# An adaLN, H3 and SwiGLU kernel: another written order, other buffer homes, and additions exchanged between VectorE and GpSimd in the front

## The chip, the cores and the metric

The kernel runs on one core of a Trainium2 chip. The time is the device time of one execution in microseconds (us); three timed executions and one profiled execution are shown for the kernel before. A core has TensorE (matmuls, PE in the profile), VectorE (DVE), ScalarE (ACT), GpSimd (POOL) and SyncE (SP). Here SP's queue issues every DMA.

## The reference

The sequence has S = 2048 steps, the model D = 512 channels, the feed-forward net F = 1792. All of it is float32.

```python
mod = silu(c) @ w_mod                       # six vectors of 512: sa, ca, ga, sb, cb, gb
h = layernorm(q) * (1 + ca) + sa
k4 = sum over t of 4 of shift_k[:, t] * k delayed by t        # per channel
kv = k4 * v
y = (causal convolution of kv with ssm_k, 2048 long, by FFT) + kv * ssm_D
x = q + ga * (h * y)
h = layernorm(x) * (1 + cb) + sb
out = x + gb * ((silu(h @ w_gate) * (h @ w_up)) @ w_down)
```

## The kernel before, in words

The kernel has two parts. The main part (lines 1755 to 1806) is a loop over weight tiles of the feed-forward net: matmuls in fp32r with operands split into a high and a low part, and sums of blocks that save one product in eight. The change doesn't touch it. The front, everything before it, is straight code: a list of 513 calls, written out by hand in `adaln_h3_swiglu`, that begins after the definitions, at line 1169.

The channels are worked on in 4 chunks of 128. In chunk 1 the four taps on k are matmuls with small diagonal matrices on TensorE (`conv`); in chunks 0, 2 and 3 they are scaled copies and additions (`tap0`, `tap`, `tap2`), and `times_v` multiplies by v. Then:

- The long convolution is a transform in two steps, of 64 points by matmuls with the table e_fwd (`er` in the profile). `kx_first` and `k_first` do the first step for the kernel ssm_k, `x_first` and `xk_first` for kv. `k_turn` and `xk_turn` turn the result on TensorE. `swap_x` and `swap_k` transpose blocks of 32x32 in place on VectorE, and `put`, `get`, `put_k`, `get_k` transpose by writing to DRAM and reading back. `skip` adds ssm_D to the first value of ssm_k.
- The second step, the product of the spectra and the step back are done in 8 half-chunks n: `x2` makes two forms of x, `x_sum` adds them, `prod` multiplies each with k's form as it leaves PSUM, `inv` goes back. Then swaps again, and `y_pe` does the last step with e_inv (`ei`).
- Beside it run the loads and small matmuls for `mod` (`mod_load`, `mod_rows`, `mod_out`, `mod_in`, `mod_part`, `mod_T`, `mod_mix`), the first layernorm (`do_stats`, `do_aggr`), and `gate_n`, `gate_m`, `gate_a`, which make h from q in half tiles (the normalised rows, times 1 + ca, plus sa, with ga worked in).
- `y_gate` multiplies h by y as it leaves PSUM, `add_y` adds that to x. `stat`, `do_norm2a`, `norm2b`, `norm_t` and `norm_s` are the second layernorm, its transposes on TensorE, and its scaling. `op_hi` and `op_lo` split the result in two parts, `w8_hi` and `w8_lo` split the weights of the first two F blocks; `wd_mul`, `wd_hi` and `wd_lo` do so for the down weights, and `split_w` for the next blocks. `gu_pe`, `gu_act` and `gu_end` are the gate and up products of these two blocks, `diff` and `downs` follow, and then the main loop begins.

What sets the order: every engine runs its instructions in the order of the program (`InOrder`, lines 56 to 64), and the framework inserts the waits between engines. A function marked `@parts` (lines 67 to 76) is a generator: each time its call stands in the list the next part of it is issued, so that `prod(4, 2)` written twice issues its matmuls at the first place and its product from PSUM at the second. So the list of calls is the schedule. SP's queue too is in that order: a load whose buffer isn't free holds up those behind it. SP's first eight loads each have a semaphore of their own, and from the ninth on they are used again.

What sets the buffers: each tile is taken from a pool under a tag with a home, a digit from the strings in `HOMES` (lines 33 to 53), read one by one as the tiles are made:

```python
    def home_of(tag, home=None):
        return f"{tag}_{next(homes[tag]) if home is None else home}"
```

`b16`, `e8`, `r4`, `k2` and `xs` are homes in SBUF, `ps` is one of four pairs of PSUM banks. A tile waits for the last use of the one before it in its home. Just ahead of the main loop another PSUM pool is opened (`next_psum`), after which `downs` writes into its banks.

An addition or product is put on VectorE or GpSimd by an argument of its call:

```python
    def gate_a(t, half, engine=pool):
        s = S1[t][:, 2 * half : 2 * half + 2]
        engine.tensor_tensor(s, s, bcs[:, None, 0, :].to_broadcast([P, 2, D]), op=ALU.add)
```

Of the kernel before, what the change touches and what calls it, by code (L numbers as in the profile page):

```python
# [34 lines left out]
        "2503145354221253044"  # L35
    ),
    "e8": (
        "61037245103724153204326432634623634642623634"
    ),
    "r4": (  # L40
        "10420123403120210433041230421140322041104230143201423104213402143021340213140204020402"
    ),
    "k2": (
        "0210210201020102010201020102010201201201201201201200112"
    ),
    "xs": (
        "10100101"
    ),
    "ps": (
        "2023102121031201321023103203102103120312310213012012012301301302310230120312032103213213210321032102"  # L50
        "31023102310231021031232123032031312"
# [28 lines left out]
def adaln_h3_swiglu(ctx, tc, q, kT, vT, kP, vP, shk, wt, ssm, dskip, wgu, wdn, c, wmod, e_fwd, e_inv, w_c, out, out_t):  # L80
# [1025 lines left out]
    def load_c():  # L1106
        sp.dma_start(csil, c)
# [74 lines left out]
    load_ssm(2)  # L1182
    kx_first(2, 1)
    k_first(0, 3)
    load_k(0, 0)
    load_ssm(0, 0)
    kx_first(2, 2)
    tap0(0, dve, 0)
    load_c()
    skip(2, pool)  # L1190
    load_e(0)
    load_k(0, 1)
    kx_first(2, 3)
    k_first(0, 2)
    kx_first(2, 2)
    skip(0)
    load_kp(1)
    load_v(0, 0)
    load_v(0, 1)
    load_v(0, 3)  # L1200
    tap(0, 1, 0)
    load_v(0, 2)
    tap(0, 2, 0)
    k_first(0, 0)
    tap0(0, dve, 1)
    load_vp(1)
    tap(0, 3, 0)
    k_first(0, 0)
    tap(0, 1, 1)
    tap(0, 2, 1)  # L1210
    kx_first(2, 0)
    tap(0, 3, 1)
    times_v(0, 0)
    times_v(0, 3)
    k_turn(0, 2)
    kx_first(2, 0)
    times_v(0, 2)
    times_v(0, 1)
    kx_first(2, 3)
    kx_first(2, 1)  # L1220
    load_k(2)
    k_turn(0, 3)
    conv(1)
    conv(1)
    conv(1)
    k_turn(0, 3)
    load_v(2)
    load_ssm(1)
    skip(1, pool)
# [12 lines left out]
    x_first(0, 1)
    x_first(0, 2)
    tap0(2, dve)
    tap(2, 1)
    tap(2, 2)
    tap2(2, 3, 1)
    x_first(0, 0)
    x_first(0, 3)
    k_turn(0, 0)  # L1250
    x_first(0, 2)
    x_first(0, 1)
    x_first(0, 3)
# [36 lines left out]
    silu_c()  # L1290
    times_v(2, 3)
    x2(1, 1)
    k_first(1, 3)
    x2(1, 1)
    x_sum(0, dve)
    load_x(1)
    prod(0, 1)
    x2(1, 2)
    x2(1, 2)
    prod(0, 0)  # L1300
    prod(0, 0)
# [72 lines left out]
    do_stats(2, 3)
    do_aggr(0)
    mod_out()
    x2(2, 2)
    x_sum(2)
    skip(3, pool)
    x2(3, 2)  # L1380
    get_k(2, 0, 1)
    x2(3, 1)
    x2(3, 1)
    xk_turn(2, 2)
    xk_turn(2, 2)
    mod_in()
    xk_turn(2, 0)
    x_sum(3)
    get_k(2, 2, 3)
    times_v(3, 2)  # L1390
    times_v(3, 0)
    do_stats(1, 3)
    xk_turn(2, 0)
    xk_turn(2, 3)
    times_v(3, 3)
    do_aggr(1)
    do_aggr(1)
# [12 lines left out]
    do_aggr(0)  # L1410
    do_aggr(0)
    do_stats(2, 2)
    times_v(3, 1, pool)
    prod(3, 2)
    prod(3, 0)
    gate_n(0, 3)
    do_stats(3, 1)
    x_first(3, 2)
    x_first(3, 2)
    gate_n(0, 2)  # L1420
    x_first(3, 3)
    x_first(3, 3)
    xk_turn(2, 1)
    xk_turn(2, 1)
    do_aggr(3)
    do_stats(2, 0)
    do_aggr(1)
    do_aggr(3)
    inv(3)
    put(0)  # L1430
    gate_n(0, 0)
    gate_n(0, 1)
    inv(3)
    inv(3)
    mod_mix()
    inv(2)
    gate_m(0, 0)
    inv(2)
    inv(2)
    x_turn(3, 0)  # L1440
    put(1)
    gate_m(0, 1, dve)
    x2(5, 2)
    do_aggr(2)
    do_aggr(2)
    x_turn(3, 0)
    x2(5, 2)
    x2(5, 1)
    get(0)
    do_aggr(2)  # L1450
    x2(5, 1)
    x_sum(5, dve)
    get(1)
# [24 lines left out]
    k_first(3, 0)
    x_first(3, 1)
    x_sum(4)  # L1480
    prod(4, 1)
    gate_m(3, 0, dve)
    k_first(3, 0)
    swap_x(12)
    k_first(3, 2)
    gate_n(2, 2)
    k_first(3, 2)
    load_einv()
    prod(4, 2)
    prod(4, 0)  # L1490
    prod(4, 2)
    gate_n(2, 0)
    prod(4, 0)
    swap_x(14)
    gate_n(1, 2)
    inv(5)
    swap_x(15)
    swap_x(13)
    gate_m(2, 1)
    gate_n(2, 1)  # L1500
    gate_n(1, 3)
    inv(5)
    gate_n(1, 0)
    inv(5)
    inv(4)
    k_turn(3, 1)
    inv(4)
    gate_m(1, 1, dve)
    gate_a(1, 1, dve)
    k_turn(3, 3)  # L1510
    inv(4)
    k_turn(3, 3)
    put(2)
    gate_a(3, 0, dve)
    gate_a(2, 1)
    gate_a(0, 0)
    gate_m(1, 0, dve)
    gate_a(1, 0, dve)
    k_turn(3, 1)
    k_turn(3, 2)  # L1520
    k_turn(3, 2)
    k_turn(3, 0)
    k_turn(3, 0)
    x2(6, 1)
    load_w(1)
    x2(6, 1)
    x2(7, 2)
    x2(7, 2)
    x2(6, 2)
    x2(7, 1)  # L1530
    prod(6, 0)
    x2(6, 2)
    x2(7, 1)
    get(2)
    gate_n(3, 3)
    gate_a(0, 1)
    x_sum(6, dve)
    prod(6, 0)
    y_pe(0, 0, 1)
    y_gate(0, 0, 1)  # L1540
    prod(7, 0)
    x_sum(7)
    prod(7, 0)
    prod(7, 1)
    prod(7, 1)
    prod(6, 2)
    prod(6, 2)
    prod(7, 2)
    add_y(0, 0, 4, (0, 1), pool)
    prod(7, 2)  # L1550
    prod(6, 1)
    gate_m(2, 0)
    prod(6, 1)
    inv(7)
    inv(7)
    w8_hi(1)
    inv(7)
    gate_a(2, 0)
    inv(6)
    stat(0, 0)  # L1560
    gate_m(3, 1)
    swap_x(14)
    mod_load(3, 4)
    w8_lo(1, pool)
    load_einv2()
    y_pe(0, 2)
# [12 lines left out]
    mod_part(4)
    mod_T(3)  # L1580
    y_gate(1, 0, 1)
    swap_x(12)
    y_pe(0, 3)
    add_y(0, 0, 4, (2,), pool)
    add_y(1, 0, 4, (0, 1), pool)
    stat(0, 1)
    y_gate(0, 3)
    mod_T(3)
    add_y(0, 0, 4, (3,), dve)
    load_w(0)  # L1590
# [299 lines left out]
```

## Time and profile before

| What | us |
|---|---|
| timed runs | 585.79, 586.29, 587.15 |
| their median | 586.29 |
| profiled execution | 587.44 |
| its span in the profile | 585.7 |
| its mean granted TensorE clock | 0.997 of full speed |

In the profile's rows `PE`, `PEld` (weight loads of TensorE), `DVE`, `ACT`, `POOL` and `SPq` name the engines or queues. All instructions recorded by `InOrder` carry line 64, so a group of instructions is told by its tiles: `out<-in` gives the names of the tile that is written and of those read. `kt` is k or its transform, `u` the sum of taps, `vt` v, `s` the half tiles of h, `bcs` the rows from `mod`, `xs` the forms of x, `X`, `T`, `K` the transformed chunks, `y` the last step of the convolution, `n` the normalised rows, `nt` their transposes, `hraw` the scaled rows, `op` the split operands, `g` the gate and up products, `dn` the down products, `a` the first products of the main part. In timeline rows the first number is the start in us from the start of the span, the second the time up to the end of the last instruction of the group, and in brackets stands the idle time before it and what ended it. In grouped rows stand the count, the busy time in us and the mean of one in ns, and then the idle time before.

### The profile page before, as it was taken

What the parts mean: (1) busy time and instruction counts of PE and PEld (TensorE: products, weight loads), DVE (VectorE), ACT (ScalarE), POOL (GpSimd) and SP (SyncE); (2) the same over time, 40 slices, a digit from 0 to 9 for tenths busy, and PEclk for the clock granted to TensorE, in tenths of its full rate; (3) what the DMA queues carried; (4) which work ended last, traced back from release to release, by engine and by line L of the source; (5) the groups of instructions that cost most, each with busy time, mean ns of one, the idle gap of its engine ahead of it and who ended that gap; (6) DMA issues with size and microseconds to landing.
All of it is one profiled execution on the core that took longest, in us unless ns stands there. A gap on an engine that the chain in (4) does not pass through costs nothing.

```text
span 585.7 us, 10169 instructions
## 1 busy us (share of the span) xinstructions
PE 568.5 (97%) x4074; PEld 447.4 (76%) x4074; DVE 447.5 (76%) x599; ACT 293.7 (50%) x440; POOL 341.1 (58%) x256
## 2 busy tenths in 40 slices
PE   3999999999999999999999999999999999999997
PEld 3994554746887888888888888888888888888885
DVE  0999975899796977877778868865577777777775
ACT  2697979954583454337354435435433333333320
POOL 0042565559364596674948794376283837474991
PEclk9999999999899999999999999999999999999999
DMA  8998999999101397191836480075343434343403
GB/s 275 413 404 304 321 177 280 379 300 350 37 37 26 149 367 284 58 355 55 290 138 205 186 304 28 5 267 196 126 162 126 161 127 161 126 161 126 162 2 143
DMA packets 41914, 113.87 MB, mean 194 GB/s; under 512 B 3189, under 2 KB 19973, under 8 KB 36362
## 3 DMA queue, kind: packets, MB, share of 16 engines
q1 hardware_dynamic: 41866, 113.22, 54.2%
q8 instruction: 32, 0.52, 0.4%
q14 instruction: 16, 0.13, 0.1%
HBM read 74.92 MB, written 38.29 MB: 193 GB/s over the span
## 4 chain that ended last, share of the span: by engine, by line
PE 87%; DVE 5%; ACT 4%; DMA 1%; issue 1%; POOL 1%; SPq 1%; ACTq 0%; DVEq 0%
PE dn L64 14%; PE b L64 12%; PE a L64 12%; PE c L64 11%; PE dq L64 10%; PE d L64 6%; PE s L64 4%; PE g L64 3%; PE iv L64 3%; PE pk L64 3%; PE px L64 2%; PE kt L64 2%; DVE xs L64 2%; DVE X L64 2%; PE y L64 1%; DMA er<-in_e_fwd 1%
## 5 line engine op out<-in xcount | busy, mean ns | idle before, releaser
L64 PE MATMUL dn<-wd,acts 128*128 128x512 f32 x336 | 83.5, 391 | 1.3 <-DVE x L64 1.1
L64 PE MATMUL b<-op,wsum 128*128 128x512 f32 x312 | 79.3, 389 | 0.0
L64 PEld LDWEIGHTS dn<-wd,acts 128*128 128x128 f32 x336 | 62.8, 188 | 15.3 <-DVE x L64 1.6
L64 POOL TENSOR_TENSOR wa<-ws,wa 128x512 fp32r<-128x512 f32 (+1 forms) x28 | 35.2, 1281 | 63.0 <-ACT wa L64 63.0
L64 PEld LDWEIGHTS b<-op,wsum 128*128 128x128 f32 x312 | 58.5, 188 | 12.4 <-ACT p L64 0.3
L64 PE MATMUL a<-op,wa 128*128 128x512 f32 x228 | 58.0, 390 | 0.0
L64 PEld LDWEIGHTS a<-op,wa 128*128 128x128 f32 x228 | 42.6, 188 | 8.8
L64 POOL TENSOR_TENSOR acts<-sg,acts 128x512 fp32r<-128x512 f32 x16 | 23.3, 1468 | 41.1 <-ACT acts L64 41.1
L64 DVE TENSOR_TENSOR x<-x,dn 128x512 f32<-128x512 f32 x56 | 37.0, 678 | 12.6 <-PE dn L64 12.5
L64 ACT ACTIVATE sg<-sg 128x512 f32<-128x512 f32 x20 | 12.7, 632 | 64.7 <-DVE sg L64 64.7
L64 PE MATMUL c<-op,wa 128*128 128x512 f32 x156 | 39.6, 389 | 0.0
L64 PE MATMUL c<-op,wsum 128*128 128x512 f32 x156 | 39.6, 389 | 0.0
L64 PE MATMUL d<-op,wsum 128*128 128x512 f32 x156 | 39.6, 389 | 0.0
L64 DVE STREAM_TRANSPOSE X<-X 128x1024 f32<-128x1024 f32 x16 | 36.8, 2360 | 2.2 <-ACT X L64 2.2
L64 POOL TENSOR_TENSOR wsum<-sr,wsum 128x1024 fp32r<-128x1024 f32 x14 | 35.6, 2542 | 0.0
L64 PEld LDWEIGHTS d<-op,wsum 128*128 128x128 f32 x156 | 29.3, 188 | 6.1
L64 PEld LDWEIGHTS c<-op,wa 128*128 128x128 f32 x156 | 29.3, 188 | 6.1
L64 PEld LDWEIGHTS c<-op,wsum 128*128 128x128 f32 x156 | 29.3, 188 | 6.1
L64 DVE TENSOR_TENSOR acc<-acc,dq 128x512 f32<-128x512 f32 x40 | 26.8, 684 | 6.8 <-PE dq L64 6.8
L64 DVE TENSOR_TENSOR xs<-pk,xs 128x1024 f32<-128x1024 f32 x24 | 28.1, 1219 | 4.8 <-POOL xs L64 2.6
L64 ACT COPY p<-a 128x512 f32<-128x512 f32 x26 | 15.4, 591 | 32.7 <-PE a L64 32.7
L64 PE MATMUL dq<-acts,wdt 128*128 128x512 f32 x120 | 30.4, 389 | 0.0
(188 smaller groups left out, 1331.7 us busy)
## 6 DMA issues: line engine op xcount, KB each, us to landing
kept<-wsum SPq DMA_DIRECT2D x12, 1024.0 KB, 7.3
wsum<-kept SPq DMA_DIRECT2D x12, 1024.0 KB, 6.5
kept<-wa SPq DMA_DIRECT2D x12, 768.0 KB, 6.0
wa<-kept SPq DMA_DIRECT2D x12, 768.0 KB, 4.3
ws<-in_wgu SPq DMA_DIRECT2D x16, 512.0 KB, 6.8
wm<-in_wmod SPq DMA_DIRECT2D x6, 1024.0 KB, 12.9
x<-in_q SPq DMA_DIRECT2D x4, 1024.0 KB, 11.5
away<-X SPq DMA_DIRECT2D x2, 2048.0 KB, 16.6
```

What stands on the lines that cost most here:

```text
L64: return lambda *a, **k: self.tc.keep_in_program_order(f(*a, **k))
```

## The change

The same 513 calls are written in another order, the home strings of the front differ, and 24 calls name another engine. The matmuls are the same ones.

The loads go in this order, before: e2, wt, ssm 0/1, e1, d, shk, ssm 0/2, ssm 0/3, e3, ssm 2, k 0/0, ssm 0/0, c, e0, k 0/1, kp 1, v 0/0, v 0/1, v 0/3, v 0/2, vp 1, k 2, v 2, ssm 1, x0, k 3, wc, mod (1, 2), x3, mod (0, 5), x1, v 3, put_k, x2, ssm 3, mod_out, get_k (0, 1), mod_in, get_k (2, 3), put 0, put 1, get 0, get 1, e_inv, put 2, w1, get 2, mod (3, 4), e_inv 2, wd0, w0, w3, w2, wd1.

After: e2, wt, ssm 0/1, e1, d, ssm 0/2, e3, ssm 0/3, ssm 2, e0, ssm 0/0, k 0/0, shk, k 0/1, kp 1, k 2, v 0/1, v 0/0, v 0/3, v 0/2, vp 1, c, ssm 1, wc, x1, x2, put_k, k 3, v 2, x0, mod (1, 2), mod (0, 5), x3, v 3, ssm 3, mod_out, get_k (2, 3), mod_in, get_k (0, 1), put 0, put 1, get 0, get 1, e_inv, put 2, w1, get 2, e_inv 2, mod (3, 4), w0, w2, wd0, w3, wd1.

Engines exchanged, `-` before and `+` after, in the order of the list (calls without an engine use the default of their function: VectorE for `skip`, `times_v` and `op_lo`, GpSimd for `x_sum`, `gate_m` and `gate_a`):

```diff
 HOMES = {
     "b16": (
-        "2503145354221253044"
+        "5421304043551253044"
     ),
     "xs": (
-        "10100101"
+        "01010101"
     ),
...
-    skip(2, pool)
+    skip(2)
-    skip(0)
+    skip(0, pool)
-    tap0(2, dve)
+    tap0(2, act)
-    times_v(2, 3)
+    times_v(2, 3, pool)
-    times_v(3, 2)
-    times_v(3, 3)
+    times_v(3, 3, pool)
+    times_v(3, 2, pool)
-    x_sum(2)
-    x_sum(3)
-    x_sum(4)
-    x_sum(7)
+    x_sum(3, dve)
+    x_sum(2, dve)
+    x_sum(4, dve)
+    x_sum(7, dve)
-    x_sum(5, dve)
-    x_sum(6, dve)
+    x_sum(5)
+    x_sum(6)
-    gate_m(0, 1, dve)
-    gate_m(1, 1, dve)
-    gate_m(1, 0, dve)
-    gate_a(1, 1, dve)
-    gate_a(3, 0, dve)
-    gate_a(1, 0, dve)
+    gate_m(0, 1)
+    gate_m(1, 1)
+    gate_m(1, 0)
+    gate_a(1, 1)
+    gate_a(3, 0)
+    gate_a(1, 0)
-    gate_m(2, 1)
-    gate_m(3, 1)
-    gate_a(0, 1)
+    gate_m(2, 1, dve)
+    gate_m(3, 1, dve)
+    gate_a(0, 1, dve)
-    add_y(0, 0, 4, (3,), dve)
+    add_y(0, 0, 4, (3,), pool)
-    w8_lo(0, dve)
+    w8_lo(0, pool)
-    op_lo("B21", pool)
+    op_lo("B21")
...
```

The order at the start, after the change (before, the second and third `k_first` were those of rows 3 and 2 of chunk 0, after `load_e(3)`; `k_turn` of chunk 0 and the taps of chunk 0 lay among `conv`):

```diff
     load_d()
-    load_shk()
-    load_ssm(0, 2)
-    load_ssm(0, 3)
     k_first(0, 1)
     k_first(0, 1)
+    load_ssm(0, 2)
     load_e(3)
-    k_first(0, 3)
+    load_ssm(0, 3)
     k_first(0, 2)
     load_ssm(2)
+    load_e(0)
+    k_first(0, 3)
+    load_ssm(0, 0)
+    skip(2)
+    load_k(0, 0)
+    load_shk()
...
```

The steps of TensorE from the last inverse operations to the feed-forward net. Before: y (0; 0, 1) between the last `prod`, then inv 7, inv 6, y (0; 2), y (1; 0, 1), mod_part 3, y (3; 0, 1), mod_part 4, mod_T 3, y (0; 3), y (1; 2, 3), mod_T 4, y (3; 2, 3), y (2; 0, 1), norm_t (0, 0), norm_t (0, 1), y (2; 2, 3), the first gu_pe. After: inv 7, inv 6, y (0; 0, 1), y (3; 0, 1), y (0; 2), y (1; 0, 1), y (2; 0, 1), y (0; 3), mod_part 3, y (1; 2, 3), mod_part 4, y (3; 2, 3), mod_T 4, mod_T 3, norm_t (0, 0), norm_t (0, 1), y (2; 2, 3), the first gu_pe.

More of the change, by code (lines that the diff above doesn't have):

```diff
@@ L1205, in adaln_h3_swiglu @@
[L1205 to L1217, printed above, removed]
+    kx_first(2, 1)
+    k_first(0, 0)
+    kx_first(2, 0)
+    kx_first(2, 3)
+    k_first(0, 0)
+    k_turn(0, 2)
+    k_turn(0, 3)
+    kx_first(2, 3)
+    tap(0, 3, 1)
+    kx_first(2, 0)
+    k_turn(0, 2)
+    k_turn(0, 0)
+    k_turn(0, 0)
+    load_v(0, 3)
@@ new lines, in adaln_h3_swiglu @@
+    x_turn(0, 1)
+    x_turn(0, 1)
+    x_first(0, 0)
+    x_first(0, 0)
+    conv(1)
+    load_c()
+    conv(1)
+    x_first(0, 2)
+    load_ssm(1)
+    load_wc()
+    x_first(0, 3)
+    x_first(0, 2)
+    x_first(0, 3)
+    x_first(0, 1)
+    x_first(1, 1)
+    tap(2, 2)
+    tap2(2, 3, 0)
+    x_first(0, 1)
+    x_first(1, 1)
+    tap2(2, 3, 1)
+    x_first(1, 2)
+    x_first(1, 2)
+    skip(1, pool)
+    x_first(1, 3)
+    x_first(1, 3)
+    k_first(1, 3)
+    k_first(1, 3)
+    k_first(1, 1)
@@ new lines, in adaln_h3_swiglu @@
+    x_first(1, 0)
+    swap_x(1)
+    x_first(1, 0)
+    k_first(1, 1)
+    load_x(1)
+    k_first(1, 0)
+    k_first(1, 2)
+    load_x(2)
+    swap_x(0)
+    k_first(1, 2)
+    swap_x(2)
+    x2(0, 2)
+    x2(0, 2)
+    put_k(2)
+    load_k(3)
+    x2(0, 1)
+    x2(0, 1)
+    tap2(2, 3, 1)
+    prod(0, 1)
+    k_first(1, 0)
+    swap_x(3)
+    x2(1, 2)
+    x_sum(0, dve)
+    do_stats(2, 2)
+    x2(1, 2)
+    load_v(2)
+    x2(1, 1)
+    x2(1, 1)
+    x_sum(1)
+    prod(0, 2)
+    prod(0, 0)
+    load_x(0)
@@ new lines, in adaln_h3_swiglu @@
+    prod(1, 1)
+    prod(0, 1)
+    prod(1, 0)
+    tap2(3, 2, 0)
+    prod(0, 2)
+    prod(0, 0)
+    prod(1, 0)
+    prod(1, 2)
+    times_v(2, 2, pool)
+    times_v(2, 3, pool)
+    prod(1, 1)
+    prod(1, 2)
+    times_v(2, 1, pool)
+    do_stats(0, 2)
+    inv(0)
+    silu_c()
+    tap0(3, act)
+    swap_x(4)
+    tap2(3, 2, 1)
+    inv(0)
+    inv(0)
+    times_v(2, 0, pool)
+    inv(1)
+    inv(1)
+    x_turn(2, 1)
+    x_turn(2, 1)
+    k_turn(1, 3)
+    k_turn(1, 0)
+    x_turn(2, 0)
+    inv(1)
@@ L1413, in adaln_h3_swiglu @@
[L1413 to L1417, printed above, removed]
+    do_stats(0, 3)
+    do_stats(2, 0)
+    do_aggr(2)
+    mod_rows()
+    do_aggr(0)
+    load_x(3)
+    do_stats(3, 3)
+    xk_first(2, 0)
+    mod_rows()
+    x2(3, 2)
+    x2(3, 2)
+    x2(2, 2)
+    x2(3, 1)
+    x2(2, 1)
+    prod(3, 1)
+    x2(3, 1)
+    x2(2, 1)
+    do_aggr(2)
+    do_stats(3, 2)
+    do_stats(3, 1)
+    do_stats(1, 0)
+    x2(2, 2)
+    do_stats(1, 2)
+    xk_turn(2, 0)
+    xk_turn(2, 0)
@@ new lines, in adaln_h3_swiglu @@
+    prod(4, 1)
+    prod(4, 1)
+    prod(5, 2)
+    prod(5, 2)
+    gate_n(0, 1)
+    gate_n(2, 2)
+    prod(5, 1)
+    prod(5, 1)
+    gate_n(0, 3)
+    prod(5, 0)
+    gate_a(3, 1)
+    prod(5, 0)
+    x_turn(3, 0)
+    get(0)
+    x_turn(3, 0)
+    k_first(3, 0)
+    k_first(3, 0)
+    k_first(3, 2)
+    k_first(3, 2)
+    gate_m(0, 1)
+    x_first(3, 0)
+    x_first(3, 1)
+    x_first(3, 0)
+    gate_a(2, 0)
+    gate_m(2, 1, dve)
+    gate_m(0, 0)
+    x_first(3, 1)
+    inv(5)
+    inv(5)
@@ L1522, in adaln_h3_swiglu @@
+    get(1)
+    k_turn(3, 3)
+    k_turn(3, 3)
+    gate_n(1, 2)
+    swap_x(13)
+    inv(4)
+    inv(4)
+    load_einv()
+    inv(4)
+    gate_a(2, 1)
     k_turn(3, 0)
+    x2(7, 2)
+    gate_a(0, 1, dve)
     k_turn(3, 0)
+    x2(7, 1)
+    put(2)
+    x2(7, 2)
+    gate_a(0, 0)
+    x2(7, 1)
+    x_sum(7, dve)
+    x2(6, 2)
+    x2(6, 2)
     x2(6, 1)
+    x2(6, 1)
+    prod(7, 0)
+    prod(7, 2)
     load_w(1)
[L1526 to L1530, printed above, removed]
-    prod(6, 0)
```

570 lines of the change are left out of this document (211 added, 359 removed).

## The prediction

> **What bounds the kernel now.** I read the page's engine table first, then the busy time by stretches, then what TensorE waited for, then TensorE's timeline at those places.
>
> ```profile
> span 585.7 us, 10169 instructions
> PE 568.5 (97%) x4074; PEld 447.4 (76%) x4074; DVE 447.5 (76%) x599; ACT 293.7 (50%) x440; POOL 341.1 (58%) x256
> ```
>
> The profiled execution took 587.44, so 1.74 lie around its span of 585.7. TensorE is busy 97% of the span, so no edit that leaves its matmuls alone can win more than the rest. The change issues the same matmuls in another order. The question is where the lost TensorE time lies. The stretches are cut where the program changes its kind of work (columns: busy time of each engine with its instructions, granted TensorE clock, DMA share, GB/s).
>
> ```profile
> core 0: us, PE busy (x) PEld busy (x) DVE busy (x) ACT busy (x) POOL busy (x), PEclk, DMA share, GB/s
> 10.88:26.47 15.59, 15.06 (x250) 14.55 (x252) 11.54 (x13) 10.30 (x14) 0.45 (x1) 1.00 1.03 408
> 26.47:73.05 46.58, 46.51 (x696) 31.50 (x694) 44.15 (x35) 40.07 (x50) 19.44 (x11) 1.00 0.94 348
> 73.05:119.00 45.95, 45.62 (x712) 27.64 (x704) 34.44 (x50) 41.30 (x53) 26.81 (x19) 1.00 0.95 274
> 119.00:143.46 24.46, 24.31 (x384) 11.82 (x384) 24.29 (x23) 11.68 (x14) 18.34 (x8) 1.00 1.00 348
> 143.46:159.65 16.19, 14.20 (x180) 13.09 (x176) 12.92 (x34) 7.92 (x11) 7.41 (x7) 0.89 0.19 68
> 146.36:149.78 3.42, 3.42 (x38) 3.42 (x34) 2.71 (x11) 1.04 (x1) 0.13 (x1) 0.50 0.00 0
> 159.65:190.46 30.81, 29.68 (x139) 24.21 (x138) 24.44 (x27) 18.88 (x26) 16.29 (x12) 1.00 0.11 36
> 190.46:585.70 395.24, 391.07 (x1739) 322.81 (x1737) 295.42 (x416) 161.22 (x273) 251.71 (x194) 1.00 0.45 166
> ```
>
> From 26.47 to 143.46 TensorE misses only 0.07, 0.33 and 0.15 us: this part can lose, hardly gain. From 143.46 to 159.65 (gates, second layernorm) it is idle for 1.99, and 3.42 us of it ran at a clock of 0.50, which costs half of that, 1.71. The next stretch misses 1.13. From 190.46 on stands the main loop, which the change doesn't touch: 395.24 in both. The waits and the timeline say what was late:
>
> ```profile
> PE s L64 <- DMA er<-in_e_fwd: 8.8, 2, 5.9
> ...
> PE y L64 <- DVE X L64: 1.0, 1, 1.0
> PE y L64 <- ACT hraw L64: 0.7, 1, 0.7
> ```
>
> ```profile
> 5.93 2.08 PE L64 MATMUL s<-er,ss 64*128 64x128 f32 x16 [5.93 <-DMA er<-in_e_fwd]
> 10.88 3.79 PE L64 MATMUL s<-er,ss 64*128 64x128 f32 x32 [2.87 <-DMA er<-in_e_fwd]
> ...
> 145.54 1.23 PE L64 MATMUL y<-X,ei 128*64 128x128 f32 x16 [1.03 <-DVE X L64]
> 146.56 1.93 PE L64 MATMUL y<-T,ei 128*64 128x128 f32 x16
> ...
> 157.76 1.09 PE L64 MATMUL y<-T,ei 128*64 128x128 f32 x16 [0.66 <-ACT hraw L64]
> ...
> 186.24 4.37 PE L64 MATMUL dn<-wd,acts 128*128 128x512 f32 x18 [1.13 <-DVE x L64]
> ```
>
> Two first loads, the last transpose of the gates, a step of the layernorm, and one addition: these are the waits worth a name. The half clock is visible in the second pair: 1.93 for 16 matmuls of y at 146.56, 1.09 for the same at 157.76.
>
> **The change, start to 26 us.** The first matmul needs the fourth load in both orders: 5.93, cost 0. The second waits at 10.88 for the ninth load, e_fwd of row 3; now the second operation is the one for row 2, whose data are the sixth load, so most of its 2.87 goes. But two operations later comes the first that needs the whole 1 MB of ssm of chunk 2, and ahead of that load stand the same transfers as before, less 8 KB of shift taps; the stretch has a DMA share of 1.03, so the order alone decides what lands when. The gain there is at most 2.87. I take 1 us of it up to the K transposes and 0.3 up to the diagonal matmuls, for which ScalarE's copies of K and T are the last, in the same number as before. What follows has ScalarE and VectorE nearly full, so I count 0 (bounds −2.9 to 0). Chunk 0's k, which now passes shift taps and c, and chunk 2's k, which passes four loads of v, don't stand on this path: their taps are needed after the K transposes only.
>
> **26 to 73 us.** tap0 of chunk 2 goes from VectorE to ScalarE, and three of its multiplications by v to GpSimd.
>
> ```profile
> L64 DVE TENSOR_SCALAR u<-kt,shk_sb 128x2048 f32<-128x2048 f32 x1 | 1.3, 1277 | 0.0
> ...
> L64 ACT ACTIVATE u<-kt,shk_sb 128x2048 f32<-128x2048 f32 x1 | 2.2, 2219 | 0.0
> ...
> L64 ACT ACT_TABLE_LOAD x2 | 2.6, 1283 | 0.7 <-PEq L1876 0.7
> ```
>
> ```profile
> 24.97 1.28 ACT L64 ACT_TABLE_LOAD   x1
> ...
> 28.86 1.99 ACT L64 COPY x<-kvt 128x1024 f32<-128x1024 f32 x2 [2.38 <-PE kvt L64]
> ```
>
> ScalarE gets 2.22 more, and the table load for SiLU, which stood at 24.97 ahead of an idle stretch of 2.38, now falls among the taps: 1.28 more. Together 3.5. ScalarE was idle for 46.58 − 40.07 = 6.5 in the stretch, 2.38 of it at 28.86, and 40.07 + 3.5 = 43.6 still fits; laid out in the new order with these durations its same set of work ends at 73.2 against 73.05. So the idle time covers it: 0. Without that cover the copies that free PSUM are 3.5 late, TensorE with them: bounds 0 to +3.5. VectorE's relief (1.28, and three times 0.69) wins nothing, since TensorE had no hole.
>
> **73 to 143 us.** Additions and products change sides between VectorE and GpSimd: six gate steps go to GpSimd and three come back, four half-sums of the inverse come to VectorE and two go, all with two inputs of 128x1024.
>
> ```profile
> L64 DVE TENSOR_TENSOR s<-s,bcs 128x1024 f32<-128x1024 f32 x7 | 8.3, 1214 | 0.1
> ...
> L64 DVE TENSOR_TENSOR x<-x,s 128x512 f32<-128x512 f32 x1 | 0.7, 692 | 0.0
> ```
>
> ```profile
> L64 POOL TENSOR_TENSOR s<-s,bcs 128x1024 f32<-128x1024 f32 x9 | 22.3, 2493 | 6.6 <-ACT s L64 6.5
> ...
> L64 POOL TENSOR_TENSOR sr<-ws 128x256 f32<-128x256 f32 x4 | 4.9, 1217 | 2.3 <-DVE wd L64 2.3
> ...
> L64 POOL TENSOR_TENSOR op<-hraw,op 128x1024 fp32r<-128x1024 f32 x1 | 3.4, 3364 | 3.3 <-ACT op L64 3.3
> ...
> L64 POOL TENSOR_TENSOR sr<-sr,ws 128x256 f32<-128x256 f32 x2 | 1.5, 740 | 0.2
> ...
> L64 POOL TENSOR_TENSOR x<-x,s 128x512 f32<-128x512 f32 x1 | 1.3, 1324 | 0.0
> ```
>
> Net, VectorE has one such step fewer (−1.2) and GpSimd one more (+2.5); with idle times of 11.5 for VectorE from 73 to 119 and 25.3 for GpSimd up to 143.46 both sides have room. VectorE is the full engine from 119 to 143.46 (24.29 of 24.46): there five gate steps leave it and one comes, 4.9 us of relief, but TensorE misses only 0.15 there, so nearly none of that can be won. Laid out in the new order with these durations, the last inverse operation ends 0.2 earlier: −0.2 (bounds −0.5 to +1.6, the last if the two-input operations of the two engines hold each other up, see the rivals). One transfer to watch:
>
> ```profile
> 116.95 0.37 SPq L64 DMA_DIRECT2D away<-T  x1
> ...
> 126.14 0.32 SPq L64 DMA_DIRECT2D T<-away  x1
> ```
>
> The third round trip through DRAM sets out 9.2 after it is put; by my walk it is put at 120.7 rather than 116.95, so it returns to be read from 129.9, and lands some 7.4 later, at 137.3. The y that needs it stands at 138.5: hidden, with 1.2 to spare. SP's queue is in order: the second e_inv (1 MB) and the two tables of mod (2 MB) wait behind it, and with 408 GB/s these 5 MB have landed by 142.2, before the first sum over mod at 144.5.
>
> **143 to 160 us.** Before, the first y pair (two groups like the one of 1.09 at 157.76, overlapping: 1.9 us) stood ahead of the last inverse operations, and now it stands behind them. VectorE's four transposes and two gates that end at 145.5 thus end at 143.6, so the 1.03 of waiting for X goes. From there the layernorm of the first half sets the end:
>
> ```profile
> L64 DVE BATCH_NORM_STATS2 bnb<-x 128x6 f32<-128x128 f32 x8 | 1.7, 296 | 0.0
> ...
> L64 POOL TENSOR_TENSOR rsb<-rsb,mhalf 128x4 f32<-128x4 f32 x2 | 2.1, 1040 | 0.2
> ...
> L64 ACT ACTIVATE n<-x,rsb 128x512 f32<-128x512 f32 x8 | 6.0, 807 | 3.2 <-DVE rsb L64 3.1
> ...
> L64 ACT ACTIVATE hraw<-nt,modT 128x512 f32<-128x512 f32 x8 | 5.8, 774 | 2.5 <-PE nt L64 2.5
> ...
> L64 ACT CAST op<-hraw 128x1024 fp32r<-128x1024 f32 x6 | 6.3, 1050 | 0.6 <-DVE hraw L64 0.5
> ...
> L64 DVE TENSOR_TENSOR op<-hraw,op 128x1024 fp32r<-128x1024 f32 x5 | 6.7, 1337 | 2.2 <-ACT op L64 2.2
> ```
>
> The last y of the first quarter runs on TensorE to 144.5, its gate to 145.4; its addition, now on GpSimd, costs 1.32 for 0.69, to 146.7; four sums at 0.30 and the aggregation to 148.8. GpSimd first ends an addition put ahead of it (149.1), then 1.04 and a small one: 150.4. Four normalisations at 0.81 to 153.5, transposes to 155.2 with the second behind the first, two scalings at 0.77 to 155.9, cast 156.9, difference 158.1. TensorE meanwhile has the other y, the sums over mod and the transposes, and starts the FFN at about 157.1 with 1 us of stall in the first group, so 158.0 in effect for 159.65: −1.7 in all, of which 0.2 came before. About as much as the half clock cost; the walk has no half clock, and three smaller waits in place of the three above. Bounds: all waits and the half clock gone, −3.7; a half clock here too, 0.
>
> The Trainium skill, "TensorE: Matmul & The Clock Gate", section "What's actually happening", has a free-running window of 4096 cycles (3413 ns) after which an idle array falls to half rate. The trace agrees with the length (3.42 at 0.50). By that rule the stretch is lost as a whole or not at all (1.71 or 0), and whether it falls can differ between runs of one kernel.
>
> **160 to 190 us.** One fp32r difference leaves GpSimd (3.36) for VectorE (1.34), one weight difference of that shape goes the other way; the addition behind the 1.13 wait stays where it is, since it waits for the new PSUM pool. I take −0.3 (bounds −1.1, the wait gone, to +1.3, the moved difference in VectorE's way).
>
> **Sum.** 0 + 0 − 0.2 − 1.5 − 0.3 + 0 = −2.0 against the profiled execution's 587.44: 585.4. That execution is above the shown runs (585.79, 586.29, 587.15). They spread by 1.36, near the 1.71 of the half clock, so some of them may have none; then the comparison is with 585.8 to 586.3, and 585.4 stands at −0.1 to −0.2%.
>
> **Rivals.**
> 1. The half clock also falls in the changed kernel: sums over mod, transposes and a short wait follow each other at 151 to 155, a place like the one where it fell before. +1.7: 587.1. Against it: the 1.03 wait just ahead of it is gone.
> 2. Slower: ScalarE becomes the bound from 26 to 73 us. The 3.5 us come where it is 86% busy; if its 6.5 us of idle time are waits for TensorE that stay, it has no room. Then 585.4 + 3.5 = 588.9. It decides as soon as TensorE shows more than 1 us of waits for kt or x copies before 73 us.
> 3. All named waits after 143 us go, with the half clock: −1.99 − 1.71 − 1.13 − 0.2 gives 587.44 − 5.0 = 582.4. For it: none of these waits is above 1.2 us. Against: the layernorm's chain now has an addition on the slower engine.
> 4. Two-input operations of VectorE and GpSimd hold each other up. For it: GpSimd's sr<-ws takes 1217 while sr<-sr,ws of the same size takes 740, so 0.48 is lost to something. Nine steps of this kind change their place on GpSimd; if three of them come to lie on VectorE's path that lay beside it before, that is +1.5: 586.9. The Trainium skill, "SBUF — State Buffer", section "Who interferes with whom", says that a VectorE instruction with two SBUF inputs and a GpSimd one that reads SBUF exclude each other for the whole instruction; by that the delay could reach a whole 1.2 each, 3.6 and 589. The trace speaks for less: the gates average 1214 on VectorE while GpSimd is at work on the same kind.
>
> **How the numbers follow.** Chances: forecast 0.40 (own range 584.2 to 586.6), half clock 0.17, ScalarE 0.15, all waits gone 0.18, the port 0.10. No change within 0.2% of 586.29 is 585.12 to 587.46, about what a measurement of this kernel can tell. Faster: all of rival 3 and 0.16 of the forecast, 0.34. Slower: ScalarE's 0.15, and 0.07 of the half clock and the port with anything beside them: 0.22. The same: 0.44. The range leaves out half of rival 3 below and two thirds of ScalarE's above: 582.8 to 588.4.
>
> **What would show it.** Right: TensorE's last inverse group ends near 134.7, the y that waited for X has no wait, the first group of g starts near 157 and the first of a near 188.5; ScalarE's table load stands behind 26 us with no TensorE wait for its copies. Wrong: a wait of TensorE above 1 us between 26 and 135, a clock under 1.00 near 151, T<-away landing after 138.5, or the main part other than 395.2.

## The result and the profile after

The changed kernel takes 583.57 us (median of 5 runs, 583.13 to 584.08); the kernel before, timed again beside it, 587.15 us (5 runs, 585.79 to 588.28). The ratio is 0.9942, 95% interval 0.9923 to 0.9960: faster by 0.58%. The forecast of 585.4 called no change the likeliest, so the sign that it thought second likeliest came true. The time lies in the stated range (582.8 to 588.4), but outside the forecast's own range (584.2 to 586.6).

The profiled execution took 583.72, its span is 581.9. What TensorE waited for up to the main part:

```profile
PE s L64 <- DMA er<-in_e_fwd: 6.6, 1, 6.6
PE y L64 <- DMA T<-away: 1.1, 1, 1.1
PE dn L64 <- DVE x L64: 0.8, 1, 0.8
PE px L64 <- ACT xk L64: 0.7, 1, 0.7
PE s L64 <- DMA ss<-in_ssm: 0.7, 2, 0.4
PE y L64 <- ACT part L64: 0.7, 1, 0.7
PE g L64 <- DVE op L64: 0.7, 1, 0.7
```

The second wait for e_fwd (2.87) is gone, and so is that for X (1.03). T<-away has come in its place with 1.1. TensorE's timeline at the same places (the last inverse operation ends at 132.94; `a` begins the main part):

```profile
13.45 2.75 PE L64 MATMUL s<-ss,er 64*128 64x128 f32 x32 [0.36 <-DMA ss<-in_ssm]
...
18.81 3.87 PE L64 MATMUL kt<-ident,kt 128*128 128x128 f32 x32
...
69.84 3.67 PE L64 MATMUL px<-X,wc 64*32 64x512 f32 x64 [0.71 <-ACT xk L64]
...
132.94 3.71 PE L64 MATMUL y<-X,ei 128*64 128x128 f32 x64
137.72 1.09 PE L64 MATMUL y<-T,ei 128*64 128x128 f32 x16 [1.07 <-DMA T<-away]
...
155.82 0.51 PE L64 MATMUL g<-op,wg 128*128 128x512 f32 x1
...
186.98 1.52 PE L64 MATMUL a<-op,wa 128*128 128x512 f32 x6
```

A new wait stands at 69.84, for ScalarE's copies `xk`. In the stretch that the prediction cut there TensorE misses 0.85 us, against 0.07 before:

```profile
26.47:73.05 46.58, 45.73 (x700) 30.39 (x704) 45.93 (x47) 41.72 (x53) 22.44 (x15) 1.00 0.90 344
```

The main part, from 186.98 to 581.90, is the same to 0.3 us. Of these, 0.23 is a wait at its last down products, which both profiles of the kernel before have and neither of the changed one has. Why it goes isn't shown. In the first profile of the kernel before:

```profile
571.62 10.27 PE L64 MATMUL dn<-acts,wd 128*128 128x512 f32 x44 [0.23 <-DVE acts L64]
```

One profile of each is not enough to share 3.8 us out, since the start differs between executions of one kernel. In the first profile of the kernel before, a step of the start, the K transposes and the end of the last inverse operation stand here:

```profile
14.46 3.90 PE L64 MATMUL s<-ss,er 64*128 64x128 f32 x48
...
20.42 0.82 PE L64 MATMUL kt<-ident,kt 128*128 128x128 f32 x5 [0.28 <-ACT kt L64]
...
136.80 1.09 PE L64 MATMUL y<-T,ei 128*64 128x128 f32 x16
```

Both kernels were profiled a second time, unaltered. The kernel before:

> The kernel before unaltered, a second profile of it, to see what of its first one belongs to the program. If the start is decided by when the loads land, its K transposes begin between 19.5 and 20.5 as in the runs that share its start. If the half clock near 146 is chance and the waits around the second layernorm are the program's, TensorE loses 6 to 8 us from the last inverse operation to the main part here too, with the half clock in another place or missing.

It took 587.39. Its TensorE timeline:

```profile
10.51 3.74 PE L64 MATMUL s<-er,ss 64*128 64x128 f32 x32 [2.42 <-DMA er<-in_e_fwd]
14.08 2.84 PE L64 MATMUL s<-ss,er 64*128 64x128 f32 x48
...
19.00 1.30 PE L64 MATMUL kt<-ident,kt 128*128 128x128 f32 x9 [0.28 <-ACT kt L64]
...
135.37 1.09 PE L64 MATMUL y<-T,ei 128*64 128x128 f32 x16
...
144.11 1.09 PE L64 MATMUL y<-X,ei 128*64 128x128 f32 x16 [1.03 <-DVE X L64]
...
152.68 0.33 PE L64 MATMUL nt<-ident,n 128*128 128x128 f32 x1 [1.10 <-ACT n L64]
...
159.56 5.95 PE L64 MATMUL g<-op,wg 128*128 128x512 f32 x24
...
190.35 1.52 PE L64 MATMUL a<-op,wa 128*128 128x512 f32 x6
```

The K transposes begin 1.4 earlier than in the first profile, and earlier than the 19.5 to 20.5 that were expected if the landing of the loads decided it. The loads account for 0.4 (10.51 for 10.88); 1.06 is the pace of the 48 matmuls behind them (2.84 for 3.90). TensorE begins slowly in both profiles: the first 16 matmuls of `s<-er,ss` take 2.08 in each, the last 16 take 1.06. How long this lasts differs between executions.

The main part begins at the same time to 0.1. The wait for X stands as it did (1.03). No half clock lies at 146: TensorE now waits for n instead, 2.1 us in four pieces, and the half clock comes later:

```profile
154.00:157.40 3.40, 3.08 (x13) 2.79 (x14) 2.94 (x10) 1.98 (x4) 1.27 (x2) 0.50 0.00 0
```

The wait for n has its cause on VectorE. There `rsb`, the last small step of the layernorm's statistics, releases ScalarE's n. In this second profile it took 2.31, because an addition on GpSimd began 0.07 ahead of it; both ended together, and n began at 151.81:

```profile
149.47 2.31 DVE L64 SCALAR_TENSOR_TENSOR rsb<-mvb,rsb 128x4 f32<-128x4 f32 x1 [0.20 <-POOL rsb L64]
...
149.40 2.35 POOL L64 TENSOR_TENSOR x<-x,s 128x1024 f32<-128x1024 f32 x1
```

In the first profile the same step took 0.15. The addition began behind it there, since the `y_gate` that it needs ended only at 152.37: VectorE had waited 1.51 for TensorE, which left the half clock at 149.78:

```profile
152.28 0.15 DVE L64 SCALAR_TENSOR_TENSOR rsb<-mvb,rsb 128x4 f32<-128x4 f32 x1
...
152.44 2.39 POOL L64 TENSOR_TENSOR x<-x,s 128x1024 f32<-128x1024 f32 x1 [1.44 <-DVE rsb L64]
```

And the changed kernel:

> The changed kernel unaltered, as the common measure for the three that run beside it. If the front is what changed, it comes out 3 to 4 us below the kernel before (583 to 584 against 586 to 588). Its first matmuls, its half-clock stretches and its wait for T<-away at y (0; 2) are looked at again: a wait near 1.1 us is expected if the round trip through DRAM is late by the program and not by chance.

It took 583.69 (6 runs, 583.29 to 585.28; ratio 0.9953, 0.9938 to 0.9967). The profiled execution took 584.87, its span is 583.1. Its timeline:

```profile
19.58 2.62 PE L64 MATMUL kt<-ident,kt 128*128 128x128 f32 x21
...
133.43 3.72 PE L64 MATMUL y<-X,ei 128*64 128x128 f32 x64
138.26 1.09 PE L64 MATMUL y<-T,ei 128*64 128x128 f32 x16 [1.12 <-DMA T<-away]
...
157.97 5.75 PE L64 MATMUL g<-op,wg 128*128 128x512 f32 x24
...
188.19 1.52 PE L64 MATMUL a<-op,wa 128*128 128x512 f32 x6
```

The wait for T<-away is the program's (1.07 and 1.12). The clock was 0.61 from 13.3 to 17.5 here: the 32 matmuls that begin at 13.41 took 3.55, against 2.75 in the first profile, and the K transposes came later.

The `rsb` step takes 0.16 in both profiles of the changed kernel, and TensorE has no wait for n:

```profile
148.95 0.16 DVE L64 SCALAR_TENSOR_TENSOR rsb<-mvb,rsb 128x4 f32<-128x4 f32 x1 [0.68 <-POOL rsb L64]
...
150.33 2.37 POOL L64 TENSOR_TENSOR x<-x,s 128x1024 f32<-128x1024 f32 x1 [1.41 <-DVE s L64]
```

The new order sees to that: `y_gate(1, 2, 3)`, which the addition needs, stood ahead of the third part of `do_norm2a(0)`, which issues `rsb`, and now stands behind it.

Shared out by stretches, with the mean of the two profiles of each kernel, and the y pair (1.9) counted to the same stretch in both:

| Stretch | before | after | difference | forecast |
|---|---|---|---|---|
| to the K transposes | 20.42, 19.00 | 18.81, 19.58 | −0.5 | −1.0, then taken back: 0 |
| to the end of the last inverse operation | 114.5, 114.5 | 114.1, 113.9 | −0.5 | −0.2 |
| to the first g | 24.7, 26.1 | 22.9, 24.5 | −1.7 | −1.5 |
| to the main part | 30.8, 30.8 | 31.2, 30.2 | −0.1 | −0.3 |
| main part | 395.2 | 394.9 | −0.3 | 0 |

The sum is −3.1; the spans (585.7 and 585.6 against 581.9 and 583.1) give −3.15. The first row rests on few executions. Other runs below have the same starts: in one with that of the kernel before the K transposes begin at 19.59, in two with that of the changed kernel at 18.79 and 18.02. With these the difference of the means is −0.9.

### The profile page after: what moved, and what is told of

It reads as the page before. It is cut to its first block, busy times and chain, and to the rows that moved or that the text cites. A ratio compares the mean times of both kernels' runs of the same rounds, so it can differ in the third digit from the quotient of the medians.

```text
span 581.9 us, 10173 instructions
## 1 busy us (share of the span) xinstructions
PE 566.4 (97%) x4074; PEld 445.5 (77%) x4074; DVE 449.2 (77%) x593; ACT 295.6 (51%) x441; POOL 349.1 (60%) x261
## 4 chain that ended last, share of the span: by engine, by line
PE 87%; DMA 5%; ACT 4%; POOL 2%; DVE 1%; issue 1%; ACTq 0%
PE dn L64 14%; PE b L64 12%; PE a L64 12%; PE c L64 12%; PE dq L64 10%; PE d L64 6%; PE s L64 4%; PE g L64 4%; PE iv L64 3%; PE pk L64 3%; PE px L64 2%; PE kt L64 2%; DMA away<-T 2%; DMA ss<-in_ssm 2%; DMA T<-away 1%; PE nt L64 1%
## 5 line engine op out<-in xcount | busy, mean ns | idle before, releaser
L64 POOL TENSOR_TENSOR s<-s,bcs 128x1024 f32<-128x1024 f32 x12 | 29.6, 2497 | 5.4 <-DVE bcs L64 5.3
L64 ACT COPY p<-a 128x512 f32<-128x512 f32 x26 | 15.4, 591 | 33.3 <-PE a L64 33.3
```

Of the source, the lines that this page charges most:

```text
L64: return lambda *a, **k: self.tc.keep_in_program_order(f(*a, **k))
```

## Experiments

All times are medians; the ratio is to the kernel before on the same chip.

| Kernel | us | ratio | 95% interval |
|---|---|---|---|
| changed, second operation late | 584.92 | 0.9963 | 0.9949 to 0.9977 |
| changed, the engines of before | 612.77 | 1.0448 | 1.0433 to 1.0463 |
| changed, y (0; 2) later | 583.00 | 0.9940 | 0.9922 to 0.9958 |
| before, second operation early | 586.94 | 0.9995 | 0.9984 to 1.0007 |
| before, with the changed tail | 591.15 | 1.0071 | 1.0057 to 1.0084 |
| before, with the changed engines | 601.62 | 1.0258 | 1.0238 to 1.0277 |
| changed, y later, ssm 2 in quarters | 582.56 | 0.9926 | 0.9913 to 0.9939 |
| changed, y later, another start | 581.48 | 0.9901 | 0.9888 to 0.9914 |
| changed, y pair put back | 584.31 | 0.9955 | 0.9943 to 0.9967 |
| changed, three gates left out | 583.40 | one run | |

**Is an early gain carried through?** First the changed kernel with its second operation late:

```diff
     load_ssm(0, 3)
-    k_first(0, 2)
+    k_first(0, 3)
     load_ssm(2)
     load_e(0)
-    k_first(0, 3)
+    k_first(0, 2)
...
-    k_first(0, 2)
+    k_first(0, 3)
...
-    k_first(0, 3)
+    k_first(0, 2)
```

> The changed kernel with rows 2 and 3 of chunk 0 exchanged in k_first, so that the second operation needs the seventh and eighth load in place of the sixth. The first theory (an early gain is carried through, since TensorE is the bound from there on) expects the second operation at about 11.0 in place of 8.6 and the time 1.5 to 2.3 us longer, with the front's end later by as much. The rival, which is the prediction's step (ScalarE and VectorE are nearly full up to 73 us and take the gain back) expects the same delay at the start and 0 to 0.3 us at the end.

The second operation began at 11.08, as both theories had it, and the time is 1.2 above the changed kernel's by medians, but the intervals overlap. Its profile takes nothing back: against the first profile of the changed kernel the K transposes begin 1.13 later (19.94) and the main part 1.06 later (188.04). The same exchange in the kernel before:

```diff
     load_e(3)
-    k_first(0, 3)
     k_first(0, 2)
+    k_first(0, 3)
...
-    k_first(0, 3)
+    k_first(0, 2)
...
-    k_first(0, 2)
+    k_first(0, 3)
```

> The kernel before with rows 2 and 3 of chunk 0 exchanged in k_first, all else as it was: the second operation then needs ssm 0/2, the seventh load, in place of e_fwd of row 3, the ninth. If an early gain is carried to the end, -0.8 to -1.5 us (the eight first operations stay bound by the 1 MB of ssm 2 that lands near 13.4). If ScalarE and VectorE take it back, as the prediction has it, 0 to -0.3.

Its K transposes began at 17.95, earlier than in either profile of the kernel before, yet the time moved by −0.05% (at most −0.16%, or −0.94 us). By the median the gain is given back, as the prediction had it; the interval leaves room for a part of it. The timeline of this run shows where it goes:

```profile
134.59 1.09 PE L64 MATMUL y<-T,ei 128*64 128x128 f32 x16
...
151.93 0.33 PE L64 MATMUL nt<-ident,n 128*128 128x128 f32 x1 [1.10 <-ACT n L64]
...
159.25 5.78 PE L64 MATMUL g<-op,wg 128*128 128x512 f32 x24
```

At the end of the inverse operations it is still 2.2 ahead of the first profile of the kernel before and 0.8 ahead of the second; the main part begins (189.88) 0.6 and 0.5 ahead. What it loses against the first profile is mainly the held step: `rsb` takes 2.31 here too, and TensorE waits 2.2 for n. Against the second profile, which has the same hold, 0.5 of 1.05 is left at the main part. So what is given back goes mainly in the layernorm's chain, not on ScalarE or VectorE up to 73 us.

Then a start that is much earlier, in the changed order. As a step towards it, ssm 2 in four loads:

```diff
-    load_ssm(2)
+    load_ssm(2, 2, 1, 0, 3)
```

> The changed kernel with y (0; 2) later, as in the run on that, and with the 1 MB load of ssm 2 cut in four of 256 KB, in the order in which kx_first needs its rows (2, 1, 0, 3). If the wait for ssm 2 at 13.4 sets the end of the eight first operations, the fourth starts near 11.5 to 12 and the K transposes 1 to 1.5 us earlier; if early gains are carried, -1.0 to -1.5 us against the run with y (0; 2) later alone, else 0.

The fourth operation began at 12.39, but the sixth waited 1.5 us for ss on GpSimd, whose addition to row 0 began at 15.4 (14.8 in the changed kernel), and the K transposes began at 18.78, no earlier. 582.56 isn't told apart from 583.00. In the next run the four operations of k_first come first:

```diff
-    load_e(2)
-    load_wt()
-    load_ssm(0, 1)
     load_e(1)
+    load_ssm(0, 1)
+    load_e(2)
+    load_ssm(0, 2)
     load_d()
...
-    load_ssm(0, 2)
     load_e(3)
     load_ssm(0, 3)
-    k_first(0, 2)
-    load_ssm(2, 2, 1, 0, 3)
     load_e(0)
-    k_first(0, 3)
+    k_first(0, 2)
     load_ssm(0, 0)
+    load_ssm(2, 2, 1, 0, 3)
+    load_wt()
+    k_first(0, 3)
     skip(2)
...
     skip(0, pool)
+    k_first(0, 0)
     kx_first(2, 2)
...
```

> The changed kernel with y (0; 2) later and another order at the start: e_fwd of row 1 and ssm 0/1 are the first two loads, the four operations of k_first come first, and ssm 2 follows in four quarters. The first matmul should start near 5.0 to 5.5 in place of 6.5 to 7.0, and the K transposes at 16.5 to 17.5 in place of 18.1 to 18.8. If an early gain is carried in the changed order, -1.0 to -2.0 us against the run with y (0; 2) later alone (583.0, so 581 to 582); if ScalarE and VectorE take it back, 0 to -0.3.

```profile
5.21 6.00 PE L64 MATMUL s<-er,ss 64*128 64x128 f32 x48 [5.21 <-DMA ss<-in_ssm]
...
16.43 3.86 PE L64 MATMUL kt<-ident,kt 128*128 128x128 f32 x32
...
25.95 2.40 PE L64 MATMUL kvt<-ident,vt 128*128 128x128 f32 x16 [0.97 <-DVE vt L64]
```

The transposes begin at 16.43, 2.35 earlier than in the run with quarters, and the time is 1.1 lower (581.48 against 582.56; 0.9901 against 0.9926, intervals that only just meet). About half of the gain is carried, and 0.9 of it by the two profiles' spans (579.9 and 580.8). The first place where some of it goes is in the last row: VectorE's product by v is now 0.97 late. So neither theory holds as it stood: what lies behind takes a part back once its slack is used up. This kernel is the fastest of all, 0.99% under the kernel before.

**Are the exchanged engines worth nothing?** The engines of before in the changed order, 24 calls (four of them shown):

```diff
-    skip(0, pool)
+    skip(0)
...
-    tap0(2, act)
+    tap0(2, dve)
...
-    x_sum(3, dve)
+    x_sum(3)
...
-    gate_a(1, 0)
+    gate_a(1, 0, dve)
```

> The changed kernel in its order and with its homes, but with all 24 exchanged calls on the engine that they had before. The prediction's step (the exchange wins nothing up to 143 us, as TensorE has no hole there) expects -0.5 to +0.5 us. The rival (VectorE, 99% busy from 26 to 73 us in the changed kernel, becomes the bound when it gets the tap and the products by v back, 3.4 us in all) expects +1.5 to +3.5 us, most of it before 93 us.

29 us longer than the changed kernel: eight times the rival's upper bound. The waits of TensorE:

```profile
PE pk L64 <- DVE xs L64: 5.8, 2, 4.5
PE s L64 <- issue: 5.5, 1, 5.5
```

The wait of 5.5 can be followed on VectorE's timeline:

```profile
16.56 0.75 DVE L64 TENSOR_SCALAR u<-kt,shk_sb 128x1024 f32<-128x1024 f32 x1 [15.27 <-DMA shk_sb<-in_shk]
...
20.53 0.27 DVE L64 TENSOR_TENSOR ss<-ss,bcs 1x128 f32<-1x128 f32 x1
```

`skip(0)`, 0.27 us of work, stands on VectorE behind four taps that wait for the shift taps, which the new load order brings late, and TensorE's k_first of row 0 waits for it. The rest was not followed up: other waits of TensorE (4.5, 3.1 and 3.0 the longest), and a mean clock of 0.983 against 1.000. The other half, the changed engines in the order of before:

```diff
-    gate_m(1, 1, dve)
-    gate_a(1, 1, dve)
+    gate_m(1, 1)
+    gate_a(1, 1)
...
-    x_sum(6, dve)
+    x_sum(6)
...
-    x_sum(7)
+    x_sum(7, dve)
```

> The kernel before in its order with the changed kernel's engine in all 24 calls. The prediction's step (exchange worth 0 up to 143 us, as TensorE has no hole) expects -0.5 to +0.5 us. The other theory, that an order and its engines are one piece (each queue is in order, so a call put on a queue behind others that wait for later data holds up all behind it, as with the engines put back in the changed kernel), expects a loss here too, +3 us or more, with waits of TensorE between 26 and 143 us.

14.5 us longer, at a mean clock of 0.988, with a wait of 7.8 for VectorE's products, which wait for GpSimd:

```profile
114.70 7.28 POOL L64 TENSOR_TENSOR s<-s,bcs 128x1024 f32<-128x1024 f32 x3 [12.96 <-ACT s L64]
123.14 10.37 POOL L64 TENSOR_TENSOR s<-s,bcs 128x1024 f32<-128x1024 f32 x4 [1.16 <-DVE s L64]
133.46 2.34 POOL L64 TENSOR_TENSOR xs<-xs 128x1024 f32<-128x1024 f32 x1
```

The half-sum at 133.46 stands behind seven gate steps. So order and engines are one piece: against the kernel before, the order alone loses 26 us and the engines alone 14, and both together win 3.

**What makes the tail shorter?** The kernel before up to its last inverse operations, and from there the changed order (banks and homes to match, and the three engines of that part):

```diff
-    y_pe(0, 0, 1)
-    y_gate(0, 0, 1)
...
-    add_y(0, 0, 4, (0, 1), pool)
...
     inv(7)
+    gate_m(3, 1)
+    gate_a(3, 1)
+    gate_a(2, 0)
...
+    inv(6)
...
+    y_pe(0, 0, 1)
+    y_gate(0, 0, 1)
...
+    y_pe(3, 0, 1)
...
```

> The kernel before up to the last inverse operations, and from there the changed kernel's order, banks and the three engines that it changes there (one addition of y and one weight difference to GpSimd, one operand difference to VectorE). By the prediction's term for 143 to 160 us: -1.5 us, -0.3 more up to 190 us, the wait for X gone, and, as the round trip through DRAM is put as early as before, no wait for T<-away. The rival (the new tail wins only because the head before it ends in another state) expects 0 or a loss.

A loss of 4 us, but in the joint, not in the tail:

```profile
132.81 7.92 PE L64 MATMUL iv<-xs,wc 32*64 32x512 f32 x96 [3.43 <-DVE xs L64]
140.66 1.53 PE L64 MATMUL y<-X,ei 128*64 128x128 f32 x24
```

Without the y pair among them, the products wait for VectorE, which has five gate steps ahead of them in the order of before. The clock falls to a half there as well (0.50 from 131.13 to 137.95): the 96 matmuls of `iv` take 7.92, against 6.51 in the kernel before. Behind the inverse operations the run takes 23.0 to the first g (140.66 to 163.66), as the changed kernel does (22.9); there is no wait for T, and `rsb` takes 0.16. So the tail keeps its length behind the old head. It isn't shown to be shorter by itself, since this head ends 3.9 and 5.3 later than in the two profiles of the kernel before, which gave the loads and the other engines that much more time.

The reverse, the changed kernel with the pair put back among the products:

```diff
+    y_pe(0, 0, 1)
     prod(6, 2)
...
+    y_gate(0, 0, 1)
     prod(6, 0)
...
-    y_pe(0, 0, 1)
-    y_gate(0, 0, 1)
```

> The changed kernel with the pair y (0; 0, 1) put back between the last products, as it stood before, and its gate with it. One theory: the changed tail wins because VectorE, freed of gates there, lets TensorE run the products without this filler, and the 1.9 us of y fill the waits for T and for the layernorm later. It expects +1.0 to +1.9 us, with TensorE idle longer between the last inverse operation and the first products of the feed-forward net. The rival (the tail wins because the wait for X and the half clock are gone, wherever the pair stands) expects 0 to +0.3.

584.31: 0.6 above the changed kernel by medians, within the intervals, and below the 1.0 to 1.9 of the first theory. The profile says why this run can't decide more:

```profile
137.71 1.09 PE L64 MATMUL y<-T,ei 128*64 128x128 f32 x16 [1.93 <-DMA T<-away]
```

The wait for T grows from 1.1 to 1.9, and y (0; 2) starts at 137.71, in the changed kernel at 137.72. The landing of T<-away sets the time in both, wherever the pair stands, and the main part begins at 186.97 and 186.98.

**The wait that was not foreseen.** y (0; 2) behind y (1; 0, 1):

```diff
     y_pe(3, 0, 1)
-    y_pe(0, 2)
-    y_gate(0, 2)
     swap_x(12)
     w8_hi(1)
     y_pe(1, 0, 1)
+    y_pe(0, 2)
     mod_load(3, 4)
+    y_gate(0, 2)
     y_gate(1, 0, 1)
```

> The changed kernel with y (0; 2), which waits 1.07 us for T<-away, behind y (1; 0, 1) and its gate behind the last transpose. If the wait is only this operation standing too early, it goes and y (0; 3) starts 1.0 earlier, at about 141.1, and with it the layernorm's chain: -0.7 to -1.0 us. If the chain from there is set by other things (the sums on VectorE, the loads for the sums over mod), the gain is 0 to 0.3.

The wait for T is gone; two smaller ones follow it (0.6 for the tables of mod, 0.4 for a gate). 583.00 against 583.69 beside it: the sign is the expected one, the size isn't resolved.

**Do VectorE and GpSimd hold each other up?** Three gate steps on GpSimd are left out, so that part of h lacks them:

```diff
-    gate_m(2, 0)
...
-    gate_a(3, 1)
...
-    gate_a(0, 0)
```

> The changed kernel without three gate steps on GpSimd: the product for rows 0 and 1 of tile 2, and the two additions for the second half of tile 3 and the first half of tile 0 are left out, so this part of h lacks them. Three gate steps on VectorE that overlapped these took 2.17, 1.91 and 2.28 us and ended 1.1 us behind GpSimd's. If the two engines hold each other up, each of the three takes 1.2 us here; if VectorE was long for another reason (a late input, PSUM), they stay at 1.9 to 2.3.

In the changed kernel the gates of that kind on VectorE averaged 1893, against 1214 before. The group there, then the same in the run without the three:

```profile
L64 DVE TENSOR_TENSOR s<-s,bcs 128x1024 f32<-128x1024 f32 x4 | 7.5, 1893 | 1.1 <-ACT s L64 1.1
```

```profile
L64 DVE TENSOR_TENSOR s<-s,bcs 128x1024 f32<-128x1024 f32 x4 | 5.4, 1380 | 1.1 <-ACT s L64 1.1
...
104.84 1.90 DVE L64 TENSOR_TENSOR s<-s,bcs 128x1024 f32<-128x1024 f32 x1
...
117.17 1.17 DVE L64 TENSOR_TENSOR s<-s,bcs 128x1024 f32<-128x1024 f32 x1
...
100.95 10.39 POOL L64 TENSOR_TENSOR s<-s,bcs 128x1024 f32<-128x1024 f32 x4
```

Two of the three fell to 1.2 (2.17 to 1.22, 2.28 to 1.17). The third stayed at 1.90, since another GpSimd gate had moved up beside it: it began 1.54 us into that one, and ended 1.09 after it. The time, 583.40 in a single run, is that of the changed kernel: TensorE wasn't waiting for these gates.

## Why the prediction was right and wrong

- **The direction** was open, and the likeliest case was wrong: no change was forecast, and it became 0.58% faster. The sum gave −2.0; the profiles give −3.1, the medians −3.6.
- **Start, the step that failed:** the 1 us up to the K transposes came about in size (−0.5 in the mean of two profiles each, −0.9 with three more, and a spread of 1.4 and 1.6 within each kernel). That it would be taken back, because "What follows has ScalarE and VectorE nearly full, so I count 0", isn't what happened in the changed kernel: a start 1.13 later moved the main part by 1.06, and of a start 2.35 earlier about half was carried. A full engine was read as an engine that sets the pace; TensorE set it, with 0.07 us missing in 46.58. Some of the reading was right: VectorE took 0.97 of the 2.35 back. In the kernel before, by the median, the gain is taken back, but mainly by the layernorm's chain behind 143 us.
- **26 to 73 us:** ScalarE took the tap and the table load (at 47.95) without a wait of TensorE for its copies of K, T or x, and rival 2 stayed under the 1 us that it had named as its sign. But the 0 was too small. TensorE waits 0.7 at 69.84 for ScalarE's copies xk, which have taps among them, in every profile with the changed order. It is the order that costs this and not the exchanged tap: the run with the engines of before has the wait too.
- **73 to 143 us:** −0.5 for −0.2 (with the stretch from the transposes on). TensorE's idle time from the transposes to the last inverse operation is no smaller than before (0.92 and 0.88 against 0.81 and 0.77), so what makes the 0.5 stays open. The slack of 1.2 for T<-away was wrong: it landed at 137.7 (137.3 was forecast), but TensorE stood there at 136.65, since the inverse operations ended at 133.0 and not at 134.7.
- **143 to 190 us** has the right size (−1.7 and −0.1 for −1.5 and −0.3) and, in good part by luck, not the right reasons. The wait for X went, but the wait for T of the same size (1.07 for 1.03) came. The half clock was priced wrongly: "costs half of that, 1.71". In the second profile it lay elsewhere, and TensorE lost 2.1 to n instead, because GpSimd's addition held VectorE's `rsb`. The timed runs of the kernel before say the same: six at a mean clock of 0.999 or 1.000 took 585.85 to 587.63, 29 at 0.996 or 0.997 took 585.76 to 587.90. Rival 1 fell in some runs only: the second profile of the changed kernel has a clock of 0.76 from 150 to 157, and there, with no hold in its place, the stretch to the first g is 1.6 longer than in the first (24.5 against 22.9). The changed order doesn't hold this step in any profile. That the hold's end makes the tail shorter is read from the profiles; no run changes it alone.
- **Rival 4** was right as a mechanism and wrong in its evidence, price and sign. The prediction said that VectorE's gates average 1214 "while GpSimd is at work on the same kind"; the five gates of 118.5 to 124.4 ran while GpSimd was idle. In the changed kernel three gates lost 2.7 together, but TensorE had no wait there, so it cost no time that these runs can show. Where it did reach TensorE is the second profile of the kernel before, at `rsb`, so that the change gains by it.
- **Engines:** to cost exchanges one by one at 1.2 against 2.5 us missed what they do in an order: 14 to 26 us when either half is taken alone.
- **Open:** what of the 1.7 in the tail belongs to which of its steps, what the place of the pair is worth, and how much of the early gain the order of before could carry with another tail.

## What to carry to other kernels

A stretch in which TensorE has no hole hands an early gain on until some engine's slack is used up, so ask how much slack each has, not whether it is busy. In a written order, which engine runs an addition decides which wait it stands behind: a 0.27 us addition cost 5.5 us behind four taps, so an order and its engines are to be changed and tested together. A short step on the critical chain can be held for the whole of another engine's addition, so look for a group member that takes many times its usual length. And before a slow stretch is priced, a second profile shows what would have taken its place.

## What the runs showed of the hardware

- VectorE's operations with both inputs in SBUF and GpSimd's additions of 128x1024 don't overlap: whichever comes second does its work after the first has ended. VectorE's additions took 1.9 to 2.3 for 1.2 and ended 1.1 behind GpSimd's; without GpSimd's they took 1.2. A step of 128x4 on VectorE, 0.15 by itself, took 2.31 (149.47) and ended with GpSimd's addition. In the changed kernel a GpSimd gate that came second, at 106.67, took 3.4 for 2.5. VectorE's products out of PSUM aren't held: two took 2.34 together at 103.63, beside a GpSimd gate. The Trainium skill, "SBUF — State Buffer", section "Who interferes with whom", states this exclusion for a VectorE instruction with two SBUF inputs and a GpSimd one that reads SBUF, and these runs agree with it.
- The half-clock stretch of about 3.4 us isn't tied to a place of the program: 146.36 to 149.78 in one execution, 154.0 to 157.4 in another of the same kernel. The free-running window of the Trainium skill, "TensorE: Matmul & The Clock Gate", section "What's actually happening", agrees with that. In the changed kernel's times one such stretch, wherever it lay, doesn't show: 583.13 to 584.08 at a mean clock of 0.999 or 1.000, 583.29 to 583.87 at 0.996 or 0.997; those at 0.994 took 584.87 and 585.28.
- The pace of the first matmuls moves the start of one kernel: 48 of them took 3.90 in one execution and 2.84 in another, of 1.4 us by which the K transposes differed (20.42 and 19.00).
